# HGRN2 attention and a maxout FFN on one core: keys of units 6 and later turned by one whole-tile stream transpose and taken through HBM

## The chip, the cores and the metric

The kernel runs on one core of a Trainium2 chip. The core has a matrix engine (TensorE, PE in the profile, with its weight loads as PEld), a vector engine (VectorE, DVE), a scalar engine (ScalarE, ACT), a general engine (GpSimd, POOL) and a sync engine (SyncE, SP) that here only issues transfers. Sixteen DMA engines move the data between HBM and the on-chip memory. The metric is device time in microseconds, the median of several executions.

## The reference

The first half is a gated linear recurrence over 768 steps, for 4 batches and 8 heads of width 48; its output is laid out by tokens and goes into a feed-forward layer with three input matrices, an elementwise maximum and an output matrix.

```python
# q, k, v, f_logit: (4, 8, 768, 48)
f = 1.0 / (1.0 + np.exp(-f_logit))
for t in range(S):
    state = f[:, :, t, :, None] * state + np.einsum('bhd,bhe->bhde', k[:, :, t], v[:, :, t])
    y[:, :, t] = np.einsum('bhd,bhde->bhe', q[:, :, t], state)
x = y.transpose(0, 2, 1, 3).reshape(3072, 384)
h = np.maximum(np.maximum(x @ w1, x @ w2), x @ w3)     # w1, w2, w3: (384, 768)
out = h @ w_out                                        # w_out: (768, 384)
```

## The kernel before

**Units.** The 768 steps are cut into 12 chunks of C = 64. A unit is one chunk of two batches, 128 tokens with all 8 heads, so there are NU = 24 units. Within a unit the recurrence is solved in closed form. Running products of the gates over the chunk (two scans on VectorE, lines 333 and 351) scale the queries and the keys, which stand with features on the partitions: 128 partitions for two heads of 64 rows each, 48 of them used. `kh` is the scaled key, `qh` the scaled query. TensorE forms the products of keys and queries of a chunk (`pairs`, L400), multiplies them with the values (`values`, L419), adds the part that comes from the state before the chunk (`finish`, L508), and forms the chunk's contribution to the new state (`sums`, L437). This last product contracts over tokens, so it needs the scaled keys once more with tokens on the partitions. That copy is `ks`, 128 tokens by 8 heads by 64.

**How keys are turned.** For units 0 to 5 TensorE turns `kh` through an identity (L371). Units 6 and later (BY_ROWS = 6) load f, k and q in blocks of 32 tokens by 32 features, eight transfers for each name and pair of units (L187), so that one stream transpose of VectorE, which turns each 32 by 32 block in place, gives the layout with features on partitions (`turned`, L300, tiles `gate`, `kt`, `qt`). For the way back, `keys_by_blocks` makes `ks` from `kh` with sixteen stream transposes on tiles of 32 partitions by 128 elements (L386), four for each quarter of the tokens. Units 22 and 23 need no `ks`, since no state follows.

**Order of the work.** The order on each engine is the order in which the program is written (a manual schedule). The loop over u runs from 4 to 23. Turn u does `values` and `sums` of unit u-1, `pairs` of unit u, `finish` of unit u-1, then the gates, keys and queries of unit n = u+1. Five calls of `fill` in each turn put in pieces of the feed-forward layer, which take most of TensorE's time. `keys_by_blocks(n, 0)` and `(n, 1)` stand near the end of turn u, `(u, 2)` and `(u, 3)` in the first half of the next. So `ks` of unit n is begun in turn n-1, finished in turn n, and read by `sums(n)` early in turn n+1.

**The queue of transfers.** Nearly all transfers go through the sync engine's queue, and each engine takes its instructions in order: a transfer that waits holds back all that follow it. In turn u stand, in this order: the packing of xT (L528, two turns in four, after `finish`), the block loads of f, k and q for unit u+3 or u+2 (all three, one name, or none, by u modulo 4), the values of unit u+2 (L164), the stores of finished rows (L564), copies that place the weights (L462 and L469, in turns 5 to 8), and one check load of a weight piece (L273). Besides an instruction's own data, a transfer waits until the one eight places before it has landed, because eight semaphores go round.

**Buffers.** `kh`, `ks` and most work tiles have two buffers. The tile `kt` has one.

## Time and profile before

| | |
|---|---|
| time, median of 3 runs | 406.63 us (406.42 to 409.85) |
| span of the profiled execution, first to last instruction | 403.7 us; the profile gives no other time of this execution, so 2.9 us of the median lie outside the span or between two executions |
| TensorE matmul, busy | 390.9 us, 97% of the span |
| VectorE, busy | 297.7 us, 74% |
| GpSimd, busy | 256.4 us, 64% |
| ScalarE, busy | 180.9 us, 45% |
| DMA packets | 181,611, of them 160,497 under 512 B; 47.21 MB |
| granted TensorE clock | 0.999 |

Busy time is the time in which an engine executes an instruction; the transfers' issue is not in it. The rows of the timeline give the start and the length in us, the engine (SPq is the sync engine's issue of transfers), the line of the kernel, the operation, what is written and read, and how many instructions the row merges. A row's group line gives the count, the total and the mean in ns of one, then the engine's idle time ahead of them and what ended it. For a transfer the group line gives how many there are, the size, and the median time from issue to landing.

### The profile page before, as it was taken

How to read it: one execution, taken by the hardware profiler on the slowest of the kernel's cores; microseconds unless marked ns; L12 is line 12 of the kernel's file. 1: busy time of each engine (PE TensorE's matmuls, PEld its weight loads, DVE VectorE, ACT ScalarE, POOL GpSimd, SP SyncE). 2: the span in 40 equal slices, each digit the busy share in tenths (PEclk: the TensorE clock that was granted, in tenths of full speed). 3: DMA queues.
4: the chain of work that ended last, by engine and by line, in shares of the span. 5: the costliest groups of instructions: out<-in, count | busy, mean ns of one | idle time of the engine just before them, and what ended most of it. 6: DMA issues, size and time to landing. Idle time of an engine off the chain costs nothing.

```text
span 403.7 us, 11683 instructions
## 1 busy us (share of the span) xinstructions
PE 390.9 (97%) x4658; PEld 339.7 (84%) x4658; DVE 297.7 (74%) x572; ACT 180.9 (45%) x431; POOL 256.4 (64%) x283
## 2 busy tenths in 40 slices
PE   5988999999999999999999999999999999999995
PEld 4766765559998889998889988899988889988995
DVE  6997897999989999897998997998995450002600
ACT  3478787422224442345532344523354425586120
POOL 2189695879997697296587277667477850435700
PEclk9999999999999999999999999999999999999999
DMA  8999986767574576576635477634573003541002
GB/s 171 233 282 284 279 214 89 153 92 150 82 96 114 69 154 135 104 120 84 131 104 97 62 113 88 156 78 81 75 157 91 1 19 87 143 136 70 2 19 63
DMA packets 181611, 47.21 MB, mean 117 GB/s; under 512 B 160497, under 2 KB 179249, under 8 KB 181553
## 3 DMA queue, kind: packets, MB, share of 16 engines
q1 hardware_dynamic: 177536, 45.52, 54.7%
q10 hardware_dynamic: 4016, 0.91, 1.1%
q8 instruction: 37, 0.61, 0.6%
q14 instruction: 22, 0.17, 0.1%
HBM read 37.75 MB, written 4.72 MB: 105 GB/s over the span
## 4 chain that ended last, share of the span: by engine, by line
PE 90%; SPq 4%; DMA 1%; ACT 1%; issue 1%; POOL 1%; DVE 0%
PE p L884 20%; PE p L633 18%; PE tr L884 16%; PE tr L633 14%; PE p L546 7%; PE y L419 3%; PE p L787 3%; PE a L400 2%; PE y L508 2%; PE a L437 2%; SPq L178 2%; DMA v_ld<-in_v_dram 1%; SPq L164 1%; SPq L222 1%; PE tr L295 1%
## 5 line engine op out<-in xcount | busy, mean ns | idle before, releaser
L386 DVE STREAM_TRANSPOSE ks<-kh 32x128 f32<-32x128 f32 x256 | 77.5, 303 | 11.5 <-POOL kh L344 7.4
L884 PE MATMUL tr<-xT,placed 128*128 128x256 f32 x180 | 44.4, 384 | 0.0
L343 POOL COPY ends<-r 128x8 f32<-128x8 f32 x24 | 8.6, 358 | 48.1 <-DVE r L333 48.1
L884 PEld LDWEIGHTS tr<-xT,placed 128*128 128x128 f32 x180 | 33.5, 190 | 4.9
L344 POOL TENSOR_TENSOR kh<-kt,r 128x512 f32<-128x512 f32 x18 | 31.9, 1772 | 8.5 <-DVE kt L300 8.5
L333 DVE TENSOR_TENSOR_SCAN r<-gate,from_one 128x520 f32<-128x520 f32 x24 | 33.2, 1382 | 5.4 <-ACT gate L312 2.8
L546 PE MATMUL p<-xT,w_in 128*128 128x256 f32 (+1 forms) x108 | 33.9, 458 | 3.0 <-POOL w_in L756 1.9
L597 POOL TENSOR_TENSOR w_in<-hm 128x256 f32<-128x256 f32 x18 | 13.3, 737 | 32.2 <-DVE hm L935 29.4
L515 ACT COPY xT<-y 64x256 f32<-64x256 f32 (+1 forms) x60 | 22.1, 368 | 22.4 <-PE y L508 21.7
L351 DVE TENSOR_TENSOR_SCAN prod<-gate,from_inv 128x520 f32<-128x520 f32 x24 | 31.6, 1317 | 0.0
L884 PE MATMUL tr<-xT,w_in 128*128 128x256 f32 x120 | 30.8, 379 | 0.0
L641 DVE TENSOR_TENSOR o<-tr,w_in 128x384 f32<-128x384 f32 (+1 forms) x11 | 5.7, 521 | 33.4 <-PE tr L633 29.0
L884 PE MATMUL p<-w_in,placed 128*128 128x256 f32 x120 | 30.4, 382 | 0.0
L633 PE MATMUL p<-placed,hm 128*128 128x192 f32 x144 | 29.7, 333 | 0.0
L546 PEld LDWEIGHTS p<-xT,w_in 128*128 128x128 f32 x108 | 19.5, 190 | 12.0 <-issue 6.0
L884 PE MATMUL p<-xT,placed 128*128 128x256 f32 x120 | 29.2, 379 | 0.0
L633 PE MATMUL tr<-w_out,w_in 128*128 128x192 f32 x144 | 28.6, 326 | 0.0
L927 DVE TENSOR_TENSOR hm<-tr,hm 128x512 f32<-128x512 f32 x15 | 10.3, 684 | 22.8 <-PE tr L884 15.9
L262 POOL TENSOR_TENSOR w_in<-top_bits,rest_bits 128x384 uint32<-128x384 uint32 x18 | 21.7, 1216 | 7.2 <-DVE top_bits L256 4.3
L884 PEld LDWEIGHTS p<-w_in,placed 128*128 128x128 f32 x120 | 22.4, 190 | 4.4 <-issue 1.5
L638 ACT COPY w_in<-p 128x384 f32<-128x384 f32 x15 | 7.2, 479 | 41.0 <-PE p L633 41.0
L284 ACT ACTIVATE raw<-top_bits 128x384 f32<-128x384 f32 x48 | 25.2, 526 | 0.4
(168 smaller groups left out, 995.6 us busy)
## 6 DMA issues: line engine op xcount, KB each, us to landing
raw<-in_moe_w_dram SPq DMA_DIRECT2D x24, 384.0 KB, 4.4
v_ld<-in_v_dram SPq DMA_DIRECT2D x48, 96.0 KB, 3.4
placed<-in_moe_w_dram SPq DMA_DIRECT2D x12, 384.0 KB, 6.3
out_dram<-o SPq DMA_DIRECT2D x45, 96.0 KB, 2.2
placed<-in_moe_w_out_dram SPq DMA_DIRECT2D x6, 384.0 KB, 5.4
f_ld<-in_f_logit_dram SPq DMA_DIRECT2D x36, 64.0 KB, 2.7
k_ld<-in_k_dram SPq DMA_DIRECT2D x36, 64.0 KB, 2.5
q_ld<-in_q_dram SPq DMA_DIRECT2D x36, 64.0 KB, 2.6
```

The costliest lines, as they stand in the source:

```text
L262: nc.gpsimd.tensor_tensor(dst, by(top), by(rest), op=ALU.add)
L284: nc.scalar.activation(over, size, AF.Relu, scale=(-1 / HI_MIN, 1.0)[step - 1], bias=(1.0, -HI_END * (1 - 2.0 ** -24))[step - 1], accum_ou ...
L333: nc.vector.tensor_tensor_scan(r[:, 0:LEN][:, ::-1], flat(gate)[:, ::-1], flat(from_one)[:, ::-1], 1.0, op0=ALU.mult, op1=ALU.max)
L344: (nc.vector if u < BY_ROWS else nc.gpsimd).tensor_tensor(kh.rearrange("p h a t -> p a h t"), kt, by_batch(r[:, 1:LEN + 1].rearrange("p (x ...
L351: nc.vector.tensor_tensor_scan(flat(prod), flat(gate_tiles[u % 2]), flat(from_inv[u % 2]), 1.0, op0=ALU.mult, op1=ALU.max)
L386: nc.vector.transpose(ks[n * 32:(n + 1) * 32, :, par, e0:e0 + 32], kh[p0:p0 + 32, :, a, t0:t0 + 32])
L419: nc.tensor.matmul(y[o:o + DP, a, hp * C:(hp + 1) * C], lhsT=v_ld[s, 2 * hp + par, :], rhs=d["at"][s, par, hp, :], start=(hp == 0), stop=F ...
L515: nc.scalar.copy(xT[o, :, t0 + a * C:t0 + (a + 1) * C], y[i, a, 0:HP * C].rearrange("p (h t) -> p h t", h=HP))
L546: nc.tensor.matmul(p if w < TOK else p.rearrange("p (two t) -> p two t", two=2), lhsT=w_in[i][:, kt, j * 128:(j + 1) * 128], rhs=x[:, t.st ...
L597: engine.tensor_tensor(dst, x, y, op=op)
L633: nc.tensor.matmul(b[:, p * HD:(p + 1) * HD], lhsT=x, rhs=w, start=id(b) not in begun, stop=True, skip_group_check=True)
L884: nc.tensor.matmul(b[:, j * HALF:(j + 1) * HALF], lhsT=w[:, (2 * n + j) * 128:(2 * n + j + 1) * 128], rhs=x, start=begin and j == 0, stop= ...
```

## The change

For units 6 to 21 the sixteen stream transposes a unit become one. `kh` is laid out by batch and head, and VectorE turns all of it at once into a new tile `by_32` (128 partitions by 8 by 2 by 32). Since a stream transpose turns blocks of 32 by 32 and leaves each block in its place, the tokens of one block then stand on 32 partitions, and blocks of the same tokens on different partition groups. The transposed operand is read as tokens of even and of odd number apart. One transfer writes the tile to a buffer in HBM (`keys_hbm`, two buffers), in rows of 64 numbers. Two transfers, one for each batch, read it back into `ks` by token rows, in pieces of 32 numbers.

`keys_turned(n)`, the transpose and the write, stands where `keys_by_blocks(n, 0)` stood, near the end of turn n-1. `keys_back(u)`, the two reads, stands where `keys_by_blocks(u, 3)` stood, in turn u, behind the load of the values of unit u+2. The new tile `by_32` is allocated under the name `kt`, which has one buffer, the same as the turned k features of the next unit.

```diff
--- before.py
+++ after.py
@@ -91,6 +91,7 @@
         ctx = ExitStack()
         with ctx:
             work = ctx.enter_context(tc.tile_pool(name="work", bufs=2))
+            hbm = ctx.enter_context(tc.tile_pool(name="hbm", bufs=2, space=bass.MemoryType.DRAM))
             ps_tr = ctx.enter_context(tc.tile_pool(name="ps_tr", bufs=2, space=bass.MemoryType.PSUM))
             ps_a = ctx.enter_context(tc.tile_pool(name="ps_a", bufs=1, space=bass.MemoryType.PSUM))
             ps_y = ctx.enter_context(tc.tile_pool(name="ps_y", bufs=1, space=bass.MemoryType.PSUM))
@@ -339,12 +340,16 @@
                 r = r_tiles[u % 2]
                 whole = r[:, 0:LEN].rearrange("p (x t) -> p x t", t=C + 1)[:, :, 1]
                 kt = features("k", u)
-                kh = work.tile([128, HP, 2, C], FP32, name="kh")
+                if u < BY_ROWS:
+                    kh = work.tile([128, HP, 2, C], FP32, name="kh")
+                else:
+                    by_batch_kh = work.tile([128, 2 * HP, C], FP32, name="kh")
+                    kh = by_batch(by_batch_kh).rearrange("p a h t -> p h a t")
                 nc.gpsimd.tensor_copy(ends[:, u, :], whole)
                 (nc.vector if u < BY_ROWS else nc.gpsimd).tensor_tensor(
                     kh.rearrange("p h a t -> p a h t"), kt,
                     by_batch(r[:, 1:LEN + 1].rearrange("p (x t) -> p x t", t=C + 1)[:, :, 1:]), op=ALU.mult)
-                ready[u] = dict(kh=kh)
+                ready[u] = dict(kh=kh, kh_by_batch=None if u < BY_ROWS else by_batch_kh)
 
             def before(u):
                 prod = work.tile([128, 2 * HP, C + 1], FP32, name="prod")
@@ -373,17 +378,24 @@
                     nc.scalar.copy(ks.rearrange("s h d -> s (h d)"), tr_s.rearrange("s a d -> s (a d)"))
                     ready[u]["ks"] = ks
 
-            def keys_by_blocks(u, n):
+            moving = {}
+
+            def keys_turned(u):
 
                 if BY_ROWS <= u < NU - 2:
-                    kh = ready[u]["kh"]
-                    if n == 0:
-                        ready[u]["ks"] = work.tile([UT, H, DP], FP32, name="ks")
-                    ks = ready[u]["ks"].rearrange("s (hp par) d -> s hp par d", par=2)
-                    a, t0 = divmod(n * 32, C)
-                    for p0 in range(0, 128, 32):
-                        par, e0 = divmod(p0, DP)
-                        nc.vector.transpose(ks[n * 32:(n + 1) * 32, :, par, e0:e0 + 32], kh[p0:p0 + 32, :, a, t0:t0 + 32])
+                    by_32 = work.tile([128, 2 * HP, 2, 32], FP32, name="kt", bufs=1)
+                    nc.vector.transpose(by_32, ready[u]["kh_by_batch"].rearrange("p x (t n) -> p x n t", n=2))
+                    moving[u] = away = hbm.tile([2, HP, 128, 2, 32], FP32, name="keys_hbm")
+                    nc.sync.dma_start(out=away.rearrange("a h p n d -> p (a h) (n d)"),
+                                      in_=by_32.rearrange("p x n d -> p x (n d)"))
+
+            def keys_back(u):
+
+                if BY_ROWS <= u < NU - 2:
+                    ready[u]["ks"] = ks = work.tile([UT, H, DP], FP32, name="ks")
+                    away = moving.pop(u).rearrange("a h (p t) n d -> a (t n) (h p) d", p=4)
+                    for a in range(2):
+                        nc.sync.dma_start(out=ks[a * C:(a + 1) * C].rearrange("s h (e d) -> s (h e) d", e=2), in_=away[a])
 
             FOUR = [(par, a) for a in range(2) for par in range(2)]
 
@@ -1085,7 +1097,6 @@
                     if n == BY_ROWS:
                         scan(n)
                     fill(part)
-                    keys_by_blocks(u, 2)
                     room_of_unit = room_of_pairs()
                     if u > GRP:
                         values(u - 1)
@@ -1112,7 +1123,7 @@
                         load(u + 3, one, "fkq" if u % GRP == 1 else "f")
                     if u + 2 < NU:
                         load_v(u + 2)
-                    keys_by_blocks(u, 3)
+                    keys_back(u)
                     if n < NU:
                         if n < BY_ROWS or n == BY_ROWS + 2:
                             sigmoids(n)
@@ -1145,9 +1156,8 @@
                         finish(u, xT)
                         pack(3, 3, xT, both)
                         packed[u // GRP] = xT
-                    keys_by_blocks(n, 0)
+                    keys_turned(n)
                     fill(part - 1000 if u < 2 * GRP else part)
-                    keys_by_blocks(n, 1)
                     check_range(u - CHECKS, 2)
                     if u + 2 >= CHECKS:
                         check_load(u + 2 - CHECKS)
```

Lines from 94 on move by one, and those behind `keys_by_blocks` by up to 12. So L386 becomes L387 (the transpose), L389 (the write) and L398 (the reads), L437 becomes L449, L508 becomes L520, L164 becomes L165, L187 L188, L273 L274, L528 L540, L564 L576.

SyncE, end of turn 9 and turn 10, before: q of unit 12, the values of units 11 and 12 (`v_ld`), the check loads (`raw`), the stores.

```order
L187 DMA q_ld_118<-in_q_dram 32x16x32
L187 DMA q_ld_118<-in_q_dram 32x16x16
L164 DMA v_ld_129<-in_v_dram 64x8x48 x2
L273 DMA raw<-in_moe_w_dram 128x3x256
L164 DMA v_ld_126<-in_v_dram 64x8x48 x2
L564 DMA out_dram<-o 64x384 x8
L273 DMA raw<-in_moe_w_dram 128x3x256
```

The same place now: the two reads of unit 9 and of unit 10 (`ks<-keys_hbm`), the writes of unit 10 and of unit 11 (`keys_hbm<-kt`).

```order
L188 DMA q_ld_120<-in_q_dram 32x16x32
L188 DMA q_ld_120<-in_q_dram 32x16x16
L165 DMA v_ld_131<-in_v_dram 64x8x48 x2
L398 DMA ks<-keys_hbm 64x16x32 x2
L389 DMA keys_hbm<-kt 128x8x64
L274 DMA raw<-in_moe_w_dram 128x3x256
L165 DMA v_ld_128<-in_v_dram 64x8x48 x2
L398 DMA ks<-keys_hbm 64x16x32 x2
L576 DMA out_dram<-o 64x384 x8
L389 DMA keys_hbm<-kt 128x8x64
L274 DMA raw<-in_moe_w_dram 128x3x256
```

Nothing that stood there has changed its order; three transfers a unit have come in between, and the reads of unit 9 stand behind the loads of unit 12 and the values of unit 11.

VectorE, turns 6 and 7 before, from the k features of unit 7 to those of unit 8: all sixteen transposes of unit 7 (`ks<-kh`), the mask on the pairs (`at`), the new state (`st`), the gates and the scan of unit 8.

```order
L300 STREAM_TRANSPOSE kt<-k_ld_117 128x512
L351 SCALAR_TENSOR_TENSOR prod<-gate_100,from_inv_97 128x520
L300 STREAM_TRANSPOSE qt<-q_ld_119 128x512
L386 STREAM_TRANSPOSE ks<-kh 32x4x32 x12
L403 TENSOR_TENSOR at<-a,mask 128x512
L452 TENSOR_TENSOR st_141<-a,state 128x384
L386 STREAM_TRANSPOSE ks<-kh 32x4x32 x4
L300 STREAM_TRANSPOSE gate_99<-sig 128x8x64
L333 SCALAR_TENSOR_TENSOR r_103<-gate_99,from_one 128x520
L336 RECIPROCAL from_inv_95<-r_103 128x8
L300 STREAM_TRANSPOSE kt<-k_ld_116 128x512
```

The same place now, with the one transpose of unit 7 (`kt<-kh`):

```order
L301 STREAM_TRANSPOSE kt<-k_ld_119 128x512
L356 SCALAR_TENSOR_TENSOR prod<-gate_102,from_inv_99 128x520
L301 STREAM_TRANSPOSE qt<-q_ld_121 128x512
L387 STREAM_TRANSPOSE kt<-kh 128x512
L415 TENSOR_TENSOR at<-a,mask 128x512
L464 TENSOR_TENSOR st_143<-a,state 128x384
L301 STREAM_TRANSPOSE gate_101<-sig 128x8x64
L334 SCALAR_TENSOR_TENSOR r_105<-gate_101,from_one 128x520
L337 RECIPROCAL from_inv_97<-r_105 128x8
L301 STREAM_TRANSPOSE kt<-k_ld_118 128x512
```

Sixteen instructions have become one at the place of the first, the rest has kept its order, and the transposes of kh and of k now write the same tile by turns.

## The prediction, written before the changed kernel was run

> **What bounds the kernel now.** I read the windows first, then what TensorE waited for, then the sync engine's queue in order of time.
>
> The page's engine line, and windows over the stage of the changed units (columns: length, then busy us of PE, PEld, DVE, ACT, POOL, the clock, the share of the 16 DMA engines, GB/s):
>
> ```profile
> PE 390.9 (97%) x4658; PEld 339.7 (84%) x4658; DVE 297.7 (74%) x572; ACT 180.9 (45%) x431; POOL 256.4 (64%) x283
> 60.00:100.00 40.00, 39.98 (x507) 26.48 (x506) 35.27 (x68) 17.63 (x41) 31.20 (x31) 1.00 0.71 119
> 175.00:233.00 58.00, 58.00 (x771) 52.73 (x770) 52.06 (x111) 24.39 (x60) 37.62 (x41) 1.00 0.57 100
> ```
>
> TensorE has no gap where units 6 to 21 are worked on: 39.98 of 40.00, then 58.00 of 58.00. VectorE is some 90% busy there, but nobody on TensorE waits for it. So the change can take next to nothing away (0.02 us of gaps in the quoted windows); the question is only whether it makes TensorE wait.
>
> What it can wait for is the sync engine's DMA queue (SPq), which issues nearly every transfer, in order. Its timeline (start, length, line, what, how many):
>
> ```profile
> 67.62 2.68 SPq L164 DMA_DIRECT2D v_ld<-in_v_dram  x4
> 70.48 1.32 SPq L462 DMA_DIRECT2D placed<-w_in  x2
> ...
> 82.81 1.42 SPq L164 DMA_DIRECT2D v_ld<-in_v_dram  x2
> 84.28 4.33 SPq L187 DMA_DIRECT2D k_ld<-in_k_dram  x8
> ...
> 108.04 2.03 SPq L528 DMA_DIRECT2D xT<-xT  x2
> 110.16 1.36 SPq L164 DMA_DIRECT2D v_ld<-in_v_dram  x2
> 111.62 4.29 SPq L187 DMA_DIRECT2D k_ld<-in_k_dram  x8
> ...
> 127.61 0.58 SPq L273 DMA_DIRECT2D raw<-in_moe_w_dram  x1
> ...
> 144.24 1.41 SPq L164 DMA_DIRECT2D v_ld<-in_v_dram  x2
> ...
> 165.58 1.34 SPq L528 DMA_DIRECT2D xT<-xT  x2
> ...
> 194.05 5.54 SPq L564 DMA_DIRECT2D out_dram<-o  x8
> ```
>
> From 67.62 to 145.65 each row starts where the one before ends, those left out too: the queue is never idle, some half a microsecond a transfer, and it runs far behind the engines. The v load at 144.24 is the one issued in turn 9 of the unit loop, whose v is for unit 11. TensorE's sums of unit 9 (L437, turn 10) had begun long before:
>
> ```profile
> 91.42 0.63 PE L437 MATMUL a<-v_ld,ks 64*64 64x48 f32 x32
> 103.63 0.63 PE L437 MATMUL a<-v_ld,ks 64*64 64x48 f32 x32
> 104.56 0.63 PE L508 MATMUL y<-qh,state 48*48 48x64 f32 x32
> 118.29 0.63 PE L437 MATMUL a<-v_ld,ks 64*64 64x48 f32 x32
> 132.67 0.63 PE L437 MATMUL a<-v_ld,ks 64*64 64x48 f32 x32
> 164.11 0.63 PE L508 MATMUL y<-qh,state 48*48 48x64 f32 x32
> 191.54 0.63 PE L437 MATMUL a<-v_ld,ks 64*64 64x48 f32 x32
> ```
>
> These are the sums of units 6, 7, 8, 9 and 13, which read ks, and the finish of units 7 and 11 (L508). Before, the queue's lag hurts nobody, since v is loaded two units ahead. ks has no such lead.
>
> **The change part by part.** *VectorE.*
>
> ```profile
> L386 DVE STREAM_TRANSPOSE ks<-kh 32x128 f32<-32x128 f32 x256 | 77.5, 303 | 11.5 <-POOL kh L344 7.4
> L300 DVE STREAM_TRANSPOSE kt<-k_ld 128x512 f32<-128x512 f32 x18 | 12.3, 686 | 1.2 <-DMA placed<-w_in 0.5 <-DMA f_ld<-in_f_logit_dram 0.3 <-DMA w_in<-w_in 0.2
> 75.39 1.24 DVE L386 STREAM_TRANSPOSE ks<-kh 32x128 f32<-32x128 f32 x4
> ```
>
> 256 instructions of 303 ns go (77.5 us), 16 whole-tile ones come. No row has this exact strided form; the same operation on 128x512 took 686 ns, so about 11 us come back, and at twice that the argument is the same. VectorE loses some 66 us of work, and TensorE gains nothing from it, having no wait to lose.
>
> *The queue.* Each of 16 units adds three transfers on SPq: one write (1024 rows of 256 B), two reads (1024 rows of 128 B each). The write needs the turned keys, the reads need the write landed, and all that is queued behind (the f, k, q and v loads, the copies of weights, the packing of xT, the stores) waits with them. Their price:
>
> ```profile
> L164 SPq DMA_DIRECT2D v_ld<-in_v_dram x48: 595/638/1730, 3.4 to 295.7; - x48
> L178 SPq DMA_DIRECT2D q_ld<-in_q_dram x5: 624/851/2833, 1.7 to 43.2; - x5
> L187 SPq DMA_DIRECT2D k_ld<-in_k_dram x72: 432/487/1957, 57.8 to 289.6; - x72
> v_ld<-in_v_dram SPq DMA_DIRECT2D x48, 96.0 KB, 3.4
> k_ld<-in_k_dram SPq DMA_DIRECT2D x5, 192.0 KB, 4.9
> k_ld<-in_k_dram SPq DMA_DIRECT2D x36, 64.0 KB, 2.5
> ```
>
> An issue is 0.49 us (512 short rows, 32 partitions), 0.64 (512 rows, 64 partitions) or 0.85 (1024 rows, under load): I take 0.75 each, bounds 0.6 and 1.2 (above the 0.85, for the crowded start). Landing from issue is 2.5, 3.4 or 4.9 us; I take 3.5, bounds 2.5 and 4.9.
>
> Now along the queue, unit by unit, with TensorE's due times from the rows above:
>
> Unit 6. Its write stands between the v loads and the first weight copy (70.48), but the keys are turned only at 75.39 + 0.7 = 76.1. The queue stands still, and the copy starts at 76.85: 6.4 late. The reads follow the v load that ended at 84.2, so at 90.7; the second is issued at 91.4 and lands at 94.9. Due 91.42: TensorE waits 3.5.
>
> Unit 7. Its reads stand ahead of the packing at 108.04: + 6.4, + 1.5 (reads of 6), + 0.75 (write of 7) = 116.7; the second lands at 120.9. Due 103.63 + 3.5 = 107.1: 13.8 more, 17.3 in all.
>
> Unit 9. After the reads and write of 7 and 8 (118.9) the packing waits for the finish of unit 7: 104.56 + 17.3, and 1.47 after the start of L508, as 165.58 is after 164.11, so 123.3. From there to the next v load's end is 3.6 (108.04 to 111.62): 126.9; reads of 8, 128.4; to the check load 16.0 (111.62 to 127.61): 144.4; write of 9, 145.15; to the end of unit 11's v 18.0 (127.61 to 145.65): 163.2. The second read lands at 163.2 + 0.75 + 3.5 = 167.5. Due 132.67 + 17.3 = 150.0: 17.5 more, 34.8 in all. Unit 8 is in time (lands at 131.2, due 118.29 + 17.3).
>
> Unit 13, and 17 four turns later. From the packing at 165.58 to the stores at 194.05 the queue is full again: 40 loads stand ahead (k and q of unit 14, f, k and q of unit 16). Added are the reads of 12 and the write of 13: the reads begin at 196.3, land at 200.55. Due 191.54: 9.0. The code's pattern repeats every four turns, so 9.0 again at unit 17; at 21 those loads have ended. The other units have reads with short ways ahead of them; 11, 15 and 19 are near.
>
> Sum of waits: 34.8 + 18.0 = 52.8. With the low bounds the same walk gives 46, with the high ones 66.
>
> *The clock behind a wait.* At the program's start, after 4.40 us without work:
>
> ```profile
> 4.40 1.08 PE L295 MATMUL tr<-ident,f_ld 128*128 128x128 f32 x4 [4.40 <-DVE q_ld L148]
> 9.29 1.05 PE L295 MATMUL p<-ident,k_ld 128*128 128x128 f32 x4
> 11.39 0.60 PE L295 MATMUL tr<-ident,f_ld 128*128 128x128 f32 x4
> ```
>
> Groups of four took 1.05 to 1.08 us for some 6 us, then 0.60: six groups, about 2.5 us lost. If each long wait is followed by that, the waits of units 6 and 7 lose nothing (the next wait, set by the queue, swallows it); those of 9, 13 and 17 add 2.4 each, 7 in all; bounds 0 and 10. The Trainium skill (TensorE: Matmul & The Clock Gate, Part 1) says that the array falls to half clock after an idle window of about 3.4 us and comes back after as long a busy one; by that, three times an estimated 1.7 us, 5 in all. No run here shows it in mid-kernel.
>
> *The tile name.* by_32 takes the name "kt", with one buffer, which the turned k features also use. So the next unit's kt waits on VectorE until the write has landed, and prod, qt and TensorE's pairs stand behind it. In turn 9 the write is issued at 144.4 and lands at 147.9, 19.6 us ahead of the reads for which TensorE stands anyway; in between lie a handful of instructions like the 0.7 us of the kt row. Covered while the reads are the later; without them it could cost a few us at unit 10.
>
> *DMA engines.*
>
> ```profile
> q1 hardware_dynamic: 177536, 45.52, 54.7%
> ```
>
> 49,152 packets come to these, some 28%: about 70% of the engines' time. Not full, so I price the issue, not the bytes.
>
> The profiled span is 403.7 us, 2.9 under the median 406.6; I put the waits on the median: 406.6 + 52.8 + 7 = 466.
>
> **The rivals.** *A, the round trip is hidden, not slower.* Between the turning of unit 6 (76.1) and its sums (91.42) lie 15 us, for a trip of two landings and three issues, some 9. If the queue had room, TensorE would never wait: 406 to 407. It decides if the reads of unit 9 can be issued by 128.4 (132.67 less 4.25); even with no added transfer the queue is there at 145.65, 17 us late. The Trainium skill (DMA: Bandwidth & Descriptors, Issuing engines are not separate DMA queues) calls issue time usually small relative to the transfer; by that rule A would hold. The trace differs in what follows: 0.49 us is small beside a landing of 2.5, yet with transfers issued back to back the queue is solid. Gain from a freer VectorE: below 1 us. 4% (3% within 1%, 1% faster).
>
> *B, fewer waits.* Only the first backlog bites, and later the stalled TensorE leaves the queue its lead: 35 us, no clock loss, 441. For: waits push all due times back. Against: the packing ties the queue to TensorE anew every four turns. 6%.
>
> *C, more.* The DMA engines fill in bursts, issues take 1.2 and landings 4.9: 66 of waits, 10 for the clock, and units 11, 15 and 19 join, whose reads also follow a packing and eight loads of f: 406.6 + 66 + 10 and a few, 485 and above. The 71% share in the first window speaks for it. 8% beyond 486.
>
> The forecast has the other 82%. Its range is 446 to 486: 452 is the low walk without the clock term, and 6 less is for issues that go faster once TensorE stands; 486 is the high walk with the clock. A measurement tells about 1% from no change: slower by more 96%, within 3%, faster 1%.
>
> **What would show it.** TensorE's sums of ks (L449 now) waiting for DMA ks<-keys_hbm, longest at units 7 and 9 (14 and 17 us), 9 at units 13 and 17, none at 8, 10, 12; SPq rows without gaps to the reads of unit 9; issues near 0.75 us; VectorE's busy time down by about 66 us; matmuls of about 1.7 times their length behind the long waits. If TensorE waits chiefly for VectorE or GpSimd, if the waits are alike at each unit, or if SPq has gaps ahead of the late reads, I am wrong in the mechanism.

## The result and the profile after

The changed kernel took 464.36 us (median of four runs, 462.31 to 465.51); the kernel before, run beside it, 406.77 us. The ratio is 1.140, with a 95% interval of 1.135 to 1.145. The forecast was 466 us, with a range of 446 to 486.

Three lines of the changed kernel's page: the engines, the clock that TensorE was granted in 40 slices of the span (463.8 us; before 403.7), in tenths, each a mean over 11.6 us, and the group of TensorE's sums that read ks.

```profile
PE 405.7 (87%) x4658; PEld 352.2 (76%) x4658; DVE 225.2 (49%) x332; ACT 180.9 (39%) x431; POOL 255.1 (55%) x283
PEclk9999999988599769999959999959999999999999
L449 PE MATMUL a<-v_ld,ks 64*64 64x48 f32 x704 | 18.1, 235 | 44.3 <-DMA ks<-keys_hbm 44.3
```

VectorE is 72.5 us less busy (297.7 to 225.2) and the span is 60.1 us longer (the medians differ by 57.6). Two readings give that sum. TensorE stood 44.3 us ahead of the sums, each time for the read-back of ks. And the same 4658 matmuls took 405.7 us of busy time where they took 390.9: 14.8 us more, because TensorE's clock, which the profile gives at full speed in all slices before, fell to half in five places. 44.3 + 14.8 = 59.1 of the 60.1 us.

The places are seen in TensorE's timeline (start, length, line, operation, how many, and in brackets the idle time before and what ended it):

```profile
93.98 0.32 PE L449 MATMUL a<-v_ld,ks 64*64 64x48 f32 x4 [1.60 <-DMA ks<-keys_hbm]
94.60 0.61 PE L449 MATMUL a<-v_ld,ks 64*64 64x48 f32 x26 [0.30 <-DMA ks<-keys_hbm]
...
120.24 0.45 PE L449 MATMUL a<-v_ld,ks 64*64 64x48 f32 x4 [11.61 <-DMA ks<-keys_hbm]
120.93 0.99 PE L449 MATMUL a<-v_ld,ks 64*64 64x48 f32 x26 [0.24 <-DMA ks<-keys_hbm]
...
165.37 1.41 PE L449 MATMUL a<-v_ld,ks 64*64 64x48 f32 x30 [12.80 <-DMA ks<-keys_hbm]
...
235.12 0.45 PE L449 MATMUL a<-v_ld,ks 64*64 64x48 f32 x4 [8.47 <-DMA ks<-keys_hbm]
236.06 0.99 PE L449 MATMUL a<-v_ld,ks 64*64 64x48 f32 x26 [0.49 <-DMA ks<-keys_hbm]
...
306.08 0.45 PE L449 MATMUL a<-v_ld,ks 64*64 64x48 f32 x4 [8.47 <-DMA ks<-keys_hbm]
```

These are units 6, 7, 9, 13 and 17. No other unit's sums waited. A whole group of 32 took 0.63 us before; behind the long waits of units 7, 9 and 13, 26 to 30 of them take 0.99 to 1.41. At unit 6 a group of 26 still takes 0.61, and the slow matmuls come after the sums.

Within the span the granted clock was 0.50 in these five stretches and 1.00 between them (start and end, length, then busy us of PE, PEld, DVE, ACT and POOL, the granted clock, the share of the DMA engines, GB/s):

```profile
95.34:98.75 3.41, 3.41 (x64) 3.27 (x56) 1.17 (x3) 1.73 (x4) 3.33 (x6) 0.50 0.74 93
112.41:126.06 13.65, 5.58 (x103) 5.31 (x104) 3.02 (x5) 1.10 (x3) 4.31 (x3) 0.50 0.52 83
156.78:170.43 13.65, 5.06 (x101) 4.45 (x102) 2.56 (x4) 1.10 (x3) 3.43 (x6) 0.50 0.88 156
231.87:242.11 10.24, 6.50 (x104) 5.60 (x105) 3.22 (x5) 1.10 (x3) 0.19 (x1) 0.50 0.81 177
300.14:313.79 13.65, 7.43 (x106) 6.35 (x107) 3.71 (x6) 1.51 (x4) 1.40 (x3) 0.50 0.75 147
```

The first stands behind the two waits of unit 6, and TensorE is busy for all of its 3.41 us. Each of the others begins 2.5 to 5.2 us after TensorE has begun to wait and ends 5.1 to 7.7 us after the sums have begun. TensorE is busy for 28.0 us of the five together; at half clock that is 14.0 us lost, nearly all of the 14.8.

Why ks is late stands in the timeline of the sync engine's queue. Here is unit 9, from its write to its reads:

```profile
144.65 0.53 SPq L389 DMA_DIRECT2D keys_hbm<-kt  x1
145.22 0.58 SPq L274 DMA_DIRECT2D raw<-in_moe_w_dram  x1
145.84 4.83 SPq L188 DMA_DIRECT2D f_ld<-in_f_logit_dram  x8
150.71 5.11 SPq L188 DMA_DIRECT2D k_ld<-in_k_dram  x8
155.87 4.21 SPq L188 DMA_DIRECT2D q_ld<-in_q_dram  x8
160.18 1.42 SPq L165 DMA_DIRECT2D v_ld<-in_v_dram  x2
161.65 1.34 SPq L398 DMA_DIRECT2D ks<-keys_hbm  x2
```

Each row starts where the one before ends. The write has been issued by 145.2; the reads are not issued until 161.65, behind 27 transfers that have nothing to do with these keys. TensorE reached the sums at 152.57 (165.37 less 12.80). The trip itself is short. The two lines by themselves (ns of an issue: least, median, most) give 0.44 and 0.65 us, and the page's DMA issues (KB each, median us from issue to landing) 3.1 and 3.4 us.

```profile
L389 SPq DMA_DIRECT2D keys_hbm<-kt x16: 367/436/1152, 77.0 to 357.0; - x16
L398 SPq DMA_DIRECT2D ks<-keys_hbm x32: 581/650/770, 90.5 to 360.6; - x32
```

```profile
keys_hbm<-kt SPq DMA_DIRECT2D x16, 256.0 KB, 3.1
ks<-keys_hbm SPq DMA_DIRECT2D x32, 128.0 KB, 3.4
```

### The profile page after: what moved, and what is told of

Same layout as the page of the kernel before. It is cut to its first block, busy times and chain, and to the rows that moved or that the text cites. A ratio compares the mean times of both kernels' runs of the same rounds, so it can differ in the third digit from the quotient of the medians.

```text
span 463.8 us, 11491 instructions
## 1 busy us (share of the span) xinstructions
PE 405.7 (87%) x4658; PEld 352.2 (76%) x4658; DVE 225.2 (49%) x332; ACT 180.9 (39%) x431; POOL 255.1 (55%) x283
## 4 chain that ended last, share of the span: by engine, by line
PE 70%; SPq 17%; DMA 6%; issue 2%; DVE 2%; ACT 2%; POOL 1%; ACTq 0%; DVEq 0%; POOLq 0%
PE p L645 14%; PE p L896 13%; PE tr L645 11%; SPq L188 11%; PE tr L896 11%; PE p L558 6%; DMA ks<-keys_hbm 4%; PE a L412 3%; PE a L449 3%; PE p L799 2%; PE y L520 2%; PE y L431 2%; SPq L165 2%; SPq L481 1%; DMA placed<-in_moe_w_dram 1%
## 5 line engine op out<-in xcount | busy, mean ns | idle before, releaser
L449 PE MATMUL a<-v_ld,ks 64*64 64x48 f32 x704 | 18.1, 235 | 44.3 <-DMA ks<-keys_hbm 44.3
L415 DVE TENSOR_TENSOR at<-a,mask 128x512 f32<-128x512 f32 x24 | 16.5, 690 | 78.5 <-PE a L412 78.4
L449 PEld LDWEIGHTS a<-v_ld,ks 64*64 64x64 f32 x704 | 15.3, 149 | 46.2 <-issue 44.2
L896 PE MATMUL tr<-xT,placed 128*128 128x256 f32 x180 | 48.7, 412 | 0.0
L348 POOL COPY ends<-r 128x8 f32<-128x8 f32 x24 | 6.9, 286 | 65.8 <-DVE r L334 65.8
L896 PEld LDWEIGHTS tr<-xT,placed 128*128 128x128 f32 x180 | 36.4, 206 | 6.1
L334 DVE TENSOR_TENSOR_SCAN r<-gate,from_one 128x520 f32<-128x520 f32 x24 | 31.4, 1307 | 5.5 <-ACT gate L313 2.9
L914 POOL TENSOR_TENSOR hm<-hm,rest_bits 128x512 f32<-128x512 f32 x15 | 21.4, 1429 | 18.5 <-ACT hm L904 18.5
L645 PE MATMUL p<-placed,hm 128*128 128x192 f32 x144 | 30.8, 341 | 0.0
L645 PE MATMUL tr<-w_out,w_in 128*128 128x192 f32 x144 | 28.6, 326 | 0.0
L558 PEld LDWEIGHTS p<-xT,w_in 128*128 128x128 f32 x108 | 19.5, 190 | 11.9 <-issue 6.0
```

Of the source, the lines that this page charges most:

```text
L334: nc.vector.tensor_tensor_scan(r[:, 0:LEN][:, ::-1], flat(gate)[:, ::-1], flat(from_one)[:, ::-1], 1.0, op0=ALU.mult, op1=ALU.max)
L415: nc.vector.tensor_tensor(at, p[:, :, 0:HP * C].rearrange("s par (h t) -> s par h t", h=HP), mask.unsqueeze(1).unsqueeze(1).to_broadcast([ ...
L449: nc.tensor.matmul(y[par * DP:(par + 1) * DP, a, Y + hp * D:Y + (hp + 1) * D], lhsT=d["ks"][s, 2 * hp + par, :], rhs=v_ld[s, 2 * hp + par, ...
L558: nc.tensor.matmul(p if w < TOK else p.rearrange("p (two t) -> p two t", two=2), lhsT=w_in[i][:, kt, j * 128:(j + 1) * 128], rhs=x[:, t.st ...
L645: nc.tensor.matmul(b[:, p * HD:(p + 1) * HD], lhsT=x, rhs=w, start=id(b) not in begun, stop=True, skip_group_check=True)
L896: nc.tensor.matmul(b[:, j * HALF:(j + 1) * HALF], lhsT=w[:, (2 * n + j) * 128:(2 * n + j + 1) * 128], rhs=x, start=begin and j == 0, stop= ...
```

## The experiments

The theory was: the loss is the place of the reads in the sync engine's queue, plus the slower clock behind each wait. The rivals were the bytes themselves, the round trip's length, the shared buffer, and VectorE's new instruction. Each run is compared with the kernel before, run on the same chip; "span" is that of the profiled execution.

One thing must be said ahead. In the profiled execution of five of the kernels (the transpose alone, all bytes without dependence, own buffer, and both with matmuls in the waits) TensorE's first group of twelve 128x512 matmuls began at 62.5 to 67.3 us, where it began at 59.9 in the changed kernel and at 59.0 before. The loads came in more slowly there: from 20 to 40 us 214 to 260 GB/s, where the changed kernel had 267 and the kernel before 280. Two of the five give prod a single buffer, which is in use that early; in the two with matmuls nothing is changed ahead of 111 us. In these two and in the transpose alone the profiled execution was also the longest of its kernel (478.52, 470.79 and 408.45 us, with medians of 473.94, 467.25 and 405.89), so a part of the late start belongs to the execution. I did not find the cause, so for the last four of the five I also give the time beyond that start, which is 403.9 us in the changed kernel (463.8 less 59.9) and 344.7 before.

### The transpose alone

```diff
-                    by_32 = work.tile([128, 2 * HP, 2, 32], FP32, name="kt", bufs=1)
+                    by_32 = work.tile([128, 2 * HP, 2, 32], FP32, name="ks")
                     nc.vector.transpose(by_32, ...)
-                    moving[u] = away = hbm.tile(...)
-                    nc.sync.dma_start(out=away..., in_=by_32...)
+                    ready[u]["ks"] = by_32.rearrange("p x n d -> p x (n d)")
```

Neither write nor reads: the sums take the turned tile as it lies, so they are of other tokens and features than the reference's.

> The whole-tile transpose alone: no write and no reads, and the sums take the turned tile as it stands in place of the keys by token rows (this leaves out the regrouping of the keys and the trip through HBM, so the result is not the reference's). VectorE keeps its saving of some 66 us. Theory (TensorE had no wait for VectorE to lose): 405.5 to 407.5 us. Rival 5 (a freer VectorE is worth something, only hidden by the trip): 403 us or less.

Measured: 405.89 us, ratio 0.998 (0.996 to 1.001). The engines' line of its page:

```profile
PE 391.6 (96%) x4658; PEld 341.3 (84%) x4658; DVE 229.5 (56%) x332; ACT 181.1 (45%) x431; POOL 261.3 (64%) x283
```

VectorE's work fell by 68 us and nothing came of it. So the new instruction costs nothing, and with the freer VectorE there is at most 0.4% to win (the interval's lower end): all of the loss is in the transfers.

### All bytes, no dependence

```diff
-                    by_32 = work.tile([128, 2 * HP, 2, 32], FP32, name="kt", bufs=1)
+                    by_32 = work.tile([128, 2 * HP, 2, 32], FP32, name="ks")
...
+                    ready[u]["ks"] = by_32.rearrange("p x n d -> p x (n d)")
...
-                    ready[u]["ks"] = ks = work.tile([UT, H, DP], FP32, name="ks")
+                    ks = work.tile([UT, H, DP], FP32, name="sink", bufs=1)
```

The transfers stay in their places; the reads go to a tile that nobody uses, and the sums take the turned tile as above, which here has the two buffers of ks and no longer shares that of kt. To make room, prod has one buffer.

> The write and both reads stay in their place on the sync engine with all their bytes, but the reads land in a tile that nobody uses, and the sums take the turned tile as it stands in place of the keys by token rows (this leaves out the regrouping of the keys, so the result is not the reference's). Theory: the queue is as full and as late, but nothing urgent stands in it; 407 to 414 us. Rival 1 (crowding by the traffic itself): 450 us or more.

Measured: 427.55 us, ratio 1.049 (1.044 to 1.054): missed by some 14 us. 8.3 us of the 22.2 by which the span is longer are the slow start. Beyond it there are 14.0 (358.7 to 344.7), with small waits on engines that hardly waited there before, for instance (engine, tile, line, then what it waited for: us, times, longest):

```profile
DVE qt L301 <- DMA q_ld<-in_q_dram: 15.0, 5, 4.0
...
PE a L413 <- POOL qh L360: 4.1, 3, 2.1
```

The first row points to how: 48 more transfers in a queue that is already behind make the loads of q late, then VectorE, GpSimd and TensorE in turn. So mere places in the queue cost up to 14 us, though the single buffer of prod may have a part in it, which this run can't separate. The dependence on ks costs the greater part.

### The buffer of its own

The turned tile no longer shares the one buffer of kt (name "k32" in place of "kt", and prod with one buffer, to make room).

> The turned tile gets a buffer of its own in place of the one it shares with the k features (room comes from one of two buffers of prod). VectorE's 15.9 us of waits for the write go. Theory: these are covered by the longer waits for ks; 460 to 466 us. Rival 3 (the shared buffer is what delays the units): 445 to 452 us.

Measured: 471.42 us, ratio 1.156 (1.150 to 1.163), some 5 us above the band; beyond the start 404.0 us, as the changed kernel's 403.9. TensorE's waits:

```profile
PE a L449 <- DMA ks<-keys_hbm: 42.2, 6, 13.8
```

In the changed kernel VectorE stood 15.9 us for the shared buffer. Without that nothing is gained: TensorE still stands 42.2 us for the reads, where it was 44.3, and 13.8 at the longest, where it was 12.8.

### The reads at the head of the turn

```diff
                     part = EARLY if u < BY_ROWS else LATER if u < 2 * GRP else PART
+                    keys_back(u)
                     if n == BY_ROWS:
...
-                    keys_back(u)
```

> Only the place of the two reads on the sync engine changes: at the head of the turn, ahead of that turn's loads. Theory: unit 6, 13 and 17 no longer wait; units 7 and 9 still do, since weight copies and loads of the turn before stand ahead of their writes (about 7 and 12 us by the walk with the measured prices), unit 10 some 4; with the clock about 435 us, 428 to 442. Rival 1 (crowded DMA engines) and rival 2 (length of the trip): 460 us or more, with the waits where they were.

Measured: 456.78 us, ratio 1.120 (1.115 to 1.126), where 435 was expected. What the sync engine and TensorE waited for:

```profile
SPq L398 <- DMA keys_hbm<-kt: 36.0, 16, 3.3
...
PE a L449 <- DMA ks<-keys_hbm: 20.5, 9, 6.9
```

The waits for ks did halve. But now each read meets its own write, not yet landed, at the head of the queue, and all that is behind it stands too: 36.0 us in 16 units, 2.3 us each. VectorE stood 63.6 us for the buffer that the turned tile shares with the k features, where it was 15.9. On TensorE other waits of up to 4.5 us came in, so that it stood 44.4 us of its span (58.1 in the changed kernel, 12.8 before), and its busy time rose to 410.6 us, 19.7 above before. Of the 23.8 us by which the waits for ks shrank, other waits took back some 10 and the clock 4.9. The expectation also missed units: 8, 14 and 18, which were to be in time, waited 2.0 to 4.4 us at their sums.

### ScalarE's queue

```diff
-                    nc.sync.dma_start(out=away..., in_=by_32...)
+            def keys_away(u):   # called one fill later
+                    nc.scalar.dma_start(out=away..., in_=by_32...)
...
-                        nc.sync.dma_start(out=ks[...]..., in_=away[a])
+                        nc.scalar.dma_start(out=ks[...]..., in_=away[a])
```

> The same transpose, write and two reads per unit, with the same bytes, but all three transfers are issued by the scalar engine; the write one fill later. Theory (the reads stand behind dozens of loads in the sync engine's in-order queue): the reads leave early, the 44 us of waits for ks go, and with them the slow clock behind them; 407 to 413 us, the margin for 16 x 3 issues in ScalarE's own order. Rival 1 (the added 8 MB and 49,000 packets crowd HBM and the DMA engines): 455 us and above. Rival 2 (the way there and back is too long in itself): waits at every unit, 430 us or more.

Measured: 439.33 us, ratio 1.076 (1.070 to 1.082), where 407 to 413 was expected. TensorE's waits for ks are all gone, yet 32 us stay. The sync engine's waits say why, and below them a row of its timeline shows one:

```profile
SPq L188 <- DMA keys_hbm<-kt: 21.2, 9, 4.5
SPq L188 <- DMA ks<-keys_hbm: 12.7, 7, 3.5
SPq L487 <- DMA keys_hbm<-kt: 7.9, 2, 4.7
SPq L165 <- DMA ks<-keys_hbm: 6.9, 3, 4.8
```

```profile
73.32 12.93 SPq L487 DMA_DIRECT2D placed<-w_in  x8
```

L188 loads f, k and q, and L487 copies weights; neither has any data in common with the keys. The eight copies of the last row took 12.93 us; such rows took 5.03 to 5.59 in the changed kernel. The compiled program shows the link (rows of the sync engine, and what each waits for):

```
L188 DMA k_ld_118<-in_k_dram 32x16x32 [waits DMAHW2_49]
L188 DMA k_ld_118<-in_k_dram 32x16x16 [waits DMAHW3_49]
L188 DMA k_ld_118<-in_k_dram 32x16x32 [waits DMAHW5_49]
```

The transfers of both queues take eight completion semaphores in turn, in an order that is fixed when the program is compiled (here number 4 went to a transfer of ScalarE's), and each waits for the last use of its own, the transfer eight before it. A transfer on ScalarE's queue that is issued late (it has to wait for VectorE, and for ScalarE's own work) therefore holds up the loads of the other queue that come eight behind it. At TensorE this arrives as waits of 8.2 us for GpSimd's qh, which needs the late loads of q, and of 10.5 us for ScalarE's copies (L656), ahead of which ScalarE had stood up to 11.6 us for a check load. So moving a transfer to another queue did not take it off the sync engine's path. This was formed after the run; the next one tests it.

### GpSimd's queue

As above, with GpSimd issuing (nc.gpsimd in place of nc.scalar). In the compiled program its transfers have completion semaphores of their own (a read: `L404 DMA ks<-keys_hbm 64x16x32 [waits DMASW0_49]`).

> All three transfers of a unit are issued from GpSimd's queue (the write one piece of the TensorE filler later than the transpose), whose completion semaphores are not those that SyncE's and ScalarE's queues take in turn. Theory (the loss is made of two couplings: reads behind SyncE's loads, and, in the run on ScalarE's queue, SyncE's loads behind ScalarE's late transfers through the shared round of eight semaphores): both are gone, no wait of TensorE for ks of more than 2 us, no wait of SyncE for keys_hbm or ks, 407 to 425 us, the upper end if an issue on GpSimd costs it several us or its products kh and qh come late behind a read that stands for its write. Rival (the bytes and the HBM round trip themselves cost the 33 us that were left on ScalarE's queue): 437 to 445 us again. Rival (a GpSimd issue is dear, GpSimd becomes the bound): over 450 us, with waits of TensorE and VectorE for qh and kh.

Measured: 416.27 us, ratio 1.021 (1.014 to 1.028), inside the band. In the sync engine's waits neither keys_hbm nor ks is left, and none of TensorE's waits is for ks. What is left of the loss (span 414.6, 10.9 above before) is on GpSimd (the group of its read issues, then TensorE's waits):

```profile
L404 POOL DMA_DIRECT2D ks<-keys_hbm x32 | 26.2, 822 | 34.0 <-DMA keys_hbm<-kt 34.0
```

```profile
PE p L651 <- POOL w_in L615: 3.1, 2, 2.2
PE tr L651 <- POOL w_in L615: 2.1, 1, 2.1
```

GpSimd stands 34.0 us with a read at its head whose write hasn't landed, and each issue takes 0.82 us of its time (0.93 a write); its product for the weights (L615) comes late, and TensorE waits 5.2 us and is busy 3.9 us longer (394.8). The same bytes over the same engines, in the same two steps through HBM, cost 9.7 us here and 57.6 in the changed kernel. So the bytes and the trip make at most about a sixth of the loss; the rest is the queue, and the semaphores shared with it.

### Which units pay

The keys of some units are turned by blocks as before, those of the others go through HBM: once units 7, 9, 13 and 17 alone (the four that waited longest), once units 8, 10, 11, 12, 14, 15, 16 and 18 to 21.

```diff
+            MOVED = (7, 9, 13, 17)        # or (8, 10, 11, 12, 14, 15, 16, 18, 19, 20, 21)
...
-                if BY_ROWS <= u < NU - 2:
+                if u in MOVED:
```

> Only units 7, 9, 13 and 17 go through HBM (4 of 16, the units whose sums waited longest). Theory (the place in the queue sets the price): waits of 6 to 12, 9 to 15, 5 to 9 and 5 to 9 us, with 2 to 4 us of lower clock behind each: 435 to 456 us. Rival (the number of transfers sets it): 4/16 of 57.6 us, about 421 us.

> Only units 8, 10, 11, 12, 14, 15, 16 and 18 to 21 go through HBM (11 of 16, the units whose sums hardly waited); units 6, 7, 9, 13 and 17 are turned by blocks as in the kernel before. Theory (the price hangs on where a unit's reads stand against the packs of loads in SyncE's queue): 406 to 416 us, waits of TensorE for ks under 6 us in all. Rival (each transfer adds its issue time to a queue that is behind, so the loss goes by the number of units): 11/16 of 57.6 us, about 446 us.

Measured: the four far units 453.95 us, ratio 1.116 (1.109 to 1.123); the eleven near ones 434.06 us, ratio 1.068 (1.060 to 1.076). TensorE's waits for ks in the first, then in the second:

```profile
114.65 1.56 PE L462 MATMUL a<-v_ld,ks 64*64 64x48 f32 x30 [10.18 <-DMA ks<-keys_hbm]
158.01 0.45 PE L462 MATMUL a<-v_ld,ks 64*64 64x48 f32 x4 [11.34 <-DMA ks<-keys_hbm]
226.94 1.51 PE L462 MATMUL a<-v_ld,ks 64*64 64x48 f32 x30 [6.88 <-DMA ks<-keys_hbm]
294.53 0.45 PE L462 MATMUL a<-v_ld,ks 64*64 64x48 f32 x4 [5.95 <-DMA ks<-keys_hbm]
```

```profile
154.58 0.45 PE L462 MATMUL a<-v_ld,ks 64*64 64x48 f32 x4 [6.00 <-DMA ks<-keys_hbm]
219.58 0.32 PE L462 MATMUL a<-v_ld,ks 64*64 64x48 f32 x4 [1.31 <-DMA ks<-keys_hbm]
...
223.29 1.10 PE L533 MATMUL y<-qh,state 48*48 48x64 f32 x32 [1.30 <-ACT seen L451]
...
284.41 0.32 PE L462 MATMUL a<-v_ld,ks 64*64 64x48 f32 x4 [1.48 <-DMA ks<-keys_hbm]
```

A quarter of the transfers makes 47.4 of the 57.6 us: the number of transfers isn't what sets the price. That rival is out. But the eleven near units cost 27.5 us where I expected nothing to 9. Units 10, 14 and 18 wait now, which never did in the changed kernel. Unit 10's write was issued at 147.75, behind 26 loads that began at 132.44, and its reads at 151.07; TensorE was at its sums at 148.58. In the changed kernel the waits of units 6, 7 and 9 had put TensorE so far back that it came to unit 10's sums at 183.13. So a unit isn't near or far by itself: whichever unit's transfers come behind the pack of loads is late, and once TensorE has been pushed back there, the units up to the next pack are in time. The two losses (27.5 and 47.4) are therefore more than the whole 57.6, and the shares of units can't be added.

Small waits cost much here: in the near units' kernel all waits of TensorE that before didn't have (9.5 for ks, 4.8 for L451) make 14.3 us, its busy time is 9.7 longer, and the span 25.4.

### Matmuls in the waits

Matmuls that nobody needs stand ahead of the sums of units 7, 9, 13 and 17, to keep TensorE busy until ks is there; the results aren't used.

```diff
+            def hold(p, n):
+                for _ in range(n):
+                    nc.tensor.matmul(p[:, 0, HP * (C + D):HP * (C + D) + 64], lhsT=ident,
+                                     rhs=from_one.rearrange("p x t -> p (x t)")[:, 0:64], start=True, stop=True)
...
+                        hold(room_of_unit, {7: 75, 9: 85, 13: 60, 17: 60}.get(u - 1, 0))
```

> As the changed kernel, with matmuls of the identity into unused columns of the pairs' bank between the values and the sums of units 7, 9, 13 and 17 (75, 85, 60 and 60 of them, some 7 to 10 us each, a little less than the waits there). Theory (the slow matmuls behind the waits are the granted clock, which falls while TensorE stands): the clock stays up, 9 us or so fewer, 453 to 459 us; the time of the reads is unchanged, so units 7 and 9 gain nothing net up to the sums of 9. Rival 4 (the matmuls behind a wait are slow for another reason, such as late operands): 464 us or more.

Measured: 473.94 us, ratio 1.163 (1.157 to 1.169), some 15 us over the band. Mis-sized: the page's group of the added matmuls and, from the timeline, one of the stretches show it:

```profile
L1006 PE MATMUL a<-from_one,ident 128*128 128x64 f32 x560 | 63.4, 276 | 0.0
```

```profile
113.44 16.96 PE L1006 MATMUL a<-from_one,ident 128*128 128x64 f32 x150
130.33 0.68 PE L449 MATMUL a<-v_ld,ks 64*64 64x48 f32 x32
```

Each took 226 ns (63.4 us over 280, each of which shows as two records), so that 63.4 us of them and 1.9 us of waits stand where 44.3 us of waits stood: 21.0 more. Yet the time beyond the start is only 8.1 more (412.0 to 403.9). The other 12.9 are the clock: the granted mean is 0.991, where the changed kernel had 0.941, and the busy time without the added matmuls is 393.0 (456.4 less 63.4), 2.1 above before in place of 14.8.

The same with 36, 42, 28 and 26 matmuls, so that they fit into the waits:

> As the earlier run with matmuls in the waits, but sized by what such a matmul took there (226 ns): 36, 42, 28 and 26 of them ahead of the sums of units 7, 9, 13 and 17, which is 8.1, 9.5, 6.3 and 5.9 us in waits of 11.9, 12.8, 9.0 and 8.7 us. Theory (some 10 to 12 us of the loss are the lower clock behind these four waits): the waits that are left are 2.5 to 4 us each, the sums of the kept time stay as they are, and the span beyond the start of the first sums falls by 6 to 11 us, so 453 to 459 us, granted clock 0.96 to 0.98. Rival (the clock has no part in the time; the slower matmuls are hidden behind later waits): 463 to 466 us. A start that is 5 to 8 us longer, as in the earlier run, would come on top of either and shows ahead of the first sums.

Measured: 467.25 us, ratio 1.145 (1.138 to 1.152). Missed again, and by the clock. TensorE's waits that are left, as in these rows of its timeline around unit 13,

```profile
235.83 0.83 PE L1006 MATMUL a<-from_one,ident 128*128 128x64 f32 x6
238.41 0.32 PE L449 MATMUL a<-v_ld,ks 64*64 64x48 f32 x4 [1.75 <-DMA ks<-keys_hbm]
239.07 0.98 PE L449 MATMUL a<-v_ld,ks 64*64 64x48 f32 x26 [0.34 <-DMA ks<-keys_hbm]
...
241.82 3.78 PE L896 MATMUL tr<-xT,placed 128*128 128x256 f32 x8
```

are 14.9 us in all, 2 to 4 in each of the five places; and the busy time without the added matmuls (438.1 less 30.3) is 407.8, 16.9 above before. Beyond the start the time is 2.3 us longer than the changed kernel's (406.2 to 403.9), where 6 to 11 less was expected. Nothing of the clock was regained: waits cut from 9 to 13 us down to 2 to 4 were followed by matmuls as slow as before (3.78 us for eight that take 1.89 at full clock).

What a place costs can be read from five kernels. The busy time above before's 390.9, by the number of places where TensorE waited for ks: changed kernel 14.8 in 5, far units 12.5 in 4, near units 9.7 in 3, fitted matmuls 16.9 in 5, reads first 19.7 in 6. That is 3.0 to 3.4 us a place on average. (It is a count over whole executions: in the two kernels with matmuls the late start has a stretch of 3.4 us at a clock of 0.50 of its own, some 1.7 us of the 16.9 and of the 2.1, and with the near units and the reads first other waits stand beside those for ks.)

The single places spread wider, taken as half of TensorE's busy time at a clock of 0.50. In the changed kernel it is 1.7 us at unit 6, with 1.9 us of waits, and 2.5 to 3.7 at the four waits of 9 to 13 us. With the fitted matmuls those four places, whose waits are now 2 to 4 us, cost 2.7 to 3.4. This is the stretch of unit 13 (columns as above):

```profile
239.07:245.90 6.83, 6.83 (x102) 5.88 (x103) 3.69 (x6) 1.36 (x4) 0.19 (x1) 0.50 0.71 166
```

## Why the prediction was right

**What bounds.** Right: TensorE had no gap to lose, and the freer VectorE was worth nothing (the transpose alone: ratio 0.998). A whole-tile transpose took 0.711 us where 0.686 was taken, and VectorE's busy time fell by 72.5 where 66 was said. The transposes make 66.2 of it (77.5 less 11.3); for the rest, other instructions of VectorE ran shorter, such as the scan r, 33.2 us before and 31.4 now.

**The queue.** The mechanism was right at each unit that it named, and the sync engine's rows have no gap from the packing at 124.61 to the reads of unit 9 at 161.65, as was said. The sizes, in us:

| unit | 6 | 7 | 9 | 13 | 17 | others | sum |
|---|---|---|---|---|---|---|---|
| wait predicted | 3.5 | 13.8 | 17.5 | 9.0 | 9.0 | 0 | 52.8 |
| wait measured | 1.9 | 11.9 | 12.8 | 9.0 | 8.7 | 0 | 44.3 |

8.5 too much. Two terms were mis-sized. An issue was priced at 0.75 us and took 0.44 (write) and 0.65 (read); a landing at 3.5, and took 3.1 and 3.4. The same walk with these gives about 50. The rest lies mostly at unit 9: the walk let TensorE arrive at 150.0, and it came at 152.6, since the slow clock behind units 6 and 7 (and 0.9 us of the start) had held it back.

**The clock.** Here the step failed in size: 7 us, with 0 to 10 as bounds, and it was 14.8. Two reasons. Half of the busy time at a clock of 0.50 is 2.5, 3.3 and 3.7 us behind units 9, 13 and 17, 9.5 in all, and not 2.4 each. And the prediction left out what stands behind units 6 and 7, as swallowed by the next wait, where it is 1.7 and 2.8. Swallowed it is, but as a shorter wait at unit 9, where the walk still counted it as waiting. So the two errors are partly one: time was put down to a wait that TensorE spent in slow matmuls. 52.8 + 7 = 59.8 and 44.3 + 14.8 = 59.1 agree better than their terms do, and the total owes that to the two errors having opposite signs. What is not the same error twice is luck: issues and landings that were priced too high made the walk 2.8 us too long, and the price behind units 9, 13 and 17 made the clock 2.5 too short. That price itself stood on weak ground. It came from slow matmuls at the program's start, and there the profile of the kernel before gives a clock of 1.00 (4.40 to 11.30 us), so those rows don't show the clock.

The Trainium skill's rule that the prediction weighed (TensorE: Matmul & The Clock Gate, Part 1) has the clock fall after an idle window of about 3.4 us. The runs differ: of the 3.4 us ahead of 95.34, where the clock fell at unit 6, TensorE had stood 1.6 + 0.3 us, and a group of six matmuls of L645 then took 2.20 us, which took 1.24 before; in the kernel with the fitted matmuls 1.75 + 0.34 us sufficed.

**The shared buffer.** Right: VectorE stood 15.9 us for it, and the kernel that gives the turned tile a buffer of its own, and prod only one, took 0.1 us more beyond the start. With the reads at the head of the turn VectorE stood 63.6 us for it; what it costs there was not run.

**The DMA engines.** Right that the bytes don't bind: the same ones on GpSimd's queue leave 9.7 of the 57.6 us. Their packets rose from 181,611 to 231,529.

**The rivals.** A (the round trip hidden) failed as the prediction said, on the queue: unit 9's reads were to be issued by 128.4 and were by 163.0. Its condition was right too: where the queue is taken out of the way (GpSimd), TensorE doesn't wait for ks at all. Under A the prediction weighed that the Trainium skill (DMA: Bandwidth & Descriptors, Issuing engines are not separate DMA queues) calls issue time usually small beside the transfer. The issues were small indeed, 0.44 and 0.65 us beside landings of 3.1 and 3.4, and it is the 27 of them in a row, with nothing able to overtake, that set the time. Of C, units 11, 15 and 19 did not wait; of B, the waits of units 13 and 17 did not go away.

**The range.** Its upper end, 486, is called the high walk with the clock, but 406.6 + 66 + 10 is 482.6. The measured time lies far below both.

**What I did not foresee** is in the experiments: that ScalarE's queue is tied to the sync engine's, that moving the reads forward makes the queue stand for the write, and that units change their parts.

Still open: why the start is 2.6 to 7.4 us later than in the changed kernel in five profiled executions, and how much of the 14 us of the transfers without dependence belongs to the single buffer of prod.

## What to carry to other kernels

A transfer that something needs soon should be priced by what stands ahead of it in its queue, not by its own length: here a trip of two landings, about 7 us, came 12.8 us late at unit 9, with 27 other transfers issued between its write and its reads. Before moving it to another queue, look whether the two queues share completion semaphores, and let no read reach the head of a queue ahead of its write's landing, whichever engine issues it. On TensorE count the waits as well as their length: shortening the waits to 2 to 4 us gave nothing of the clock back here, and only closing them did (2.1 us of busy time above before in place of 14.8); but the matmuls that closed them were longer than the waits, and the time rose.

## What was unexpected of the hardware

- Waits of 2 to 4 us on TensorE were followed by as much slow work as waits of 9 to 13 us: 2.7 to 3.4 us lost at a place against 2.5 to 3.7; only unit 6's two waits, 1.9 us together, cost 1.7. The granted clock was 1.00 or 0.50 in these traces, and the stretches at 0.50 behind the waits for ks were 3.41 us long or a whole multiple of it (6.83, 10.24 and 13.65).
- In this program the transfers of the sync engine's and ScalarE's queues were coupled by eight completion semaphores taken in turn: loads of the one stood up to 4.8 us for transfers of the other. GpSimd's were not.
- An issue of the same transfers took 0.44 (write) and 0.65 us (read) on the sync engine's queue, and 0.93 and 0.82 us on GpSimd, as work of the engine itself.
- The write of 256 KB to HBM landed 3.1 us after its issue and the reads of 128 KB, in rows of 128 B, 3.4 us after theirs; on GpSimd's queue 4.0 and 4.2.
